# Filters loaded without a hold, other warm-up matmuls, and a feed-forward in 47 blocks of 512 tokens

## The chip, the cores and the metric

The kernel runs on one core of one Trainium2 chip. The metric is device time in microseconds (us). Before the change: 983.06 us, the median of ten runs (981.53 to 984.56).

## The reference

```python
def _attn_ref(x, filt_r, filt_i):               # x: 8 x 3008 x 256, filters: 1505 x 256
    X = np.fft.rfft(x, axis=1)
    F = (filt_r + 1j * filt_i)[None, :, :]
    return np.fft.irfft(X * F, n=x.shape[1], axis=1)

def _moe_ref(x, w_gate, w_val, w_out):          # 24064 tokens, d_model 256, d_ff 1536
    gate = np.maximum(x @ w_gate, 0.0)
    val = x @ w_val
    return gate * val @ w_out
```

The second takes the first one's result as 24064 x 256. Inputs and output are float32.

## The kernel before

**The transform.** A sequence of 3008 is taken as N1 x N2 = 94 x 32, token = n1 * 32 + n2, and done in stages for each of 8 batches.
- Stage A (`items_a`, L243 to L249): a DFT over n1. 16 items, each two float32 matmuls psA of 512 columns from x in SBUF (`XF`, two halves of 16 n2 each), one copy to `asb` on ScalarE. Every fourth item stores its `asb` to DRAM (`Abuf`) by the SP queue. `load_at` reads `Abuf` back in another order into `at`, one of four slabs of 32 partitions each. This is the first bounce.
- Stage B (`items_b`, L274 to L298): 12 items of a forward matmul pair psX, products with the filters on VectorE (`tt`, `uu`), and, two items late, an inverse of four matmuls psD, copied to `dsb` on ScalarE; two more items finish the inverses. Four stores (five in batch 0) put `dsb` into DRAM (`Dbuf`). `load_d` reads it back in eight tiles `dC`, each with four values of n2. Every tile needs all the stores. This is the second bounce.
- Stage C (`item_c`, L328): the DFT back over n1 by matmuls of 94 columns, psY, copied to `yT`, the feed-forward's input.

**The feed-forward** goes in blocks. A block takes one `dC` tile: four n2, all n1, 376 tokens, and 12 steps, one for each 128 columns of d_ff. In a step `gv` (L345 to L350) makes psV and psG with two matmuls each of 376 columns, ScalarE copies psV to `vsb`, and VectorE makes `prod` of psG and `vsb`. In the same step `o_part` (L365) does three matmuls psO of 256 columns for the block before: 128, 128 and 120 tokens in turn. After its steps 7 and 11 psO is copied and written by one transfer of SP's queue: 256 rows of 1 KB, then 120. `item_c` for the next block is called after steps 6 and 10.

**The order** is written by hand; each engine runs its instructions in the order of the program. The batch ahead is worked on beside the blocks: `side` holds what is called after which step (counted from the start of the batch's 96 steps). Stage A begins at step 5 (20 for batch 1), one item a step; stage B at step 35 (51), one item every two steps; `load_d` at step 66 (82). `load_x` for the batch after that is issued by POOL as soon as stage A has read a half of `XF`.

**The prologue** does batch 0 alone. x is loaded by SP, filters by POOL (`load_filters`, 20 transfers), after a hold: `hold_gpsimd` is a small copy on POOL that waits for a given tile, here for the first x. `place_filters` copies rows within SBUF, the first half on VectorE, the second by SP's transfers. Feed-forward weights come in three parts (`load_vg`) and `load_o`, by POOL: the first two parts after a hold on the third slab of `at`, the third after a hold on the first `dC`. `warm` issues junk matmuls of 512 columns, psJ, in stage A (one an item), after it (20), in stage B (two an item) and after it (26).

Of the kernel before, what the change touches and what calls it, by code (L numbers as in the profile page):

```python
# [13 lines left out]
BF16 = mybir.dt.bfloat16  # L14
# [13 lines left out]
N1, N2 = 94, 32  # L28
NROW = 96
NG = 24  # L30
S = N1 * N2
# [8 lines left out]
def _tables():  # L40
# [10 lines left out]
    lo = 32 * (lo % 32 // 8) + 8 * (lo // 32) + lo % 8  # L51
    i2t = np.zeros((128, NG, 64))
    i2u = np.zeros((128, NG, 64))
    perm = np.arange(N2) // 4 + 8 * (np.arange(N2) % 4)
    perm = np.concatenate([perm, 32 + perm])
    for hg in range(48):
        g, a = divmod(hg, 2)
        rows = slice(a * 64, a * 64 + 64)
        f = np.zeros((64, 64))
        t = np.zeros((64, 64))  # L60
        u = np.zeros((64, 64))
        k1 = 2 * hg + 2 if hg < 23 else 0 if hg == 23 else 2 * (hg - 24) + 1
        th = 2 * np.pi * ((n1 * k1) % N1) / N1
        wa[part, 2 * hg] = np.cos(th)
        if k1 not in (0, 47):
            wa[part, 2 * hg + 1] = -np.sin(th)
            m1[2 * hg] = 2.0 * np.cos(th) / S
            m1[2 * hg + 1] = -2.0 * np.sin(th) / S
            k = np.stack([k1 + N1 * p, S - (N1 * (p + 1) - k1)], 1).reshape(32)
            conj = np.tile([1.0, -1.0], 16)  # L70
            th = 2 * np.pi * (np.outer(n2, k) % S) / S
            c, s = np.cos(th), np.sin(th)
            f[:] = np.block([[c, -s], [s, c]])
            ct, st = c.T, s.T
            t[:] = np.block([[ct, st], [-st, ct]])
            u[:] = np.block([[-st, ct], [-ct, -st]]) * np.concatenate([conj, conj])[:, None]
        else:
            m1[2 * hg] = np.cos(th) / S
            th = 2 * np.pi * (np.outer(n2, k1 + N1 * p) % S) / S
            c, s = np.cos(th), np.sin(th)  # L80
            f[0:32, 0:32:2] = c
            f[0:32, 32::2] = -s
            t[0:32:2, 0:32] = 2.0 * c.T
            t[32::2, 0:32] = -2.0 * s.T
            u[0:32:2, 0:32] = -2.0 * s.T
            u[32::2, 0:32] = -2.0 * c.T
            if k1 == 0:
                sign = np.where(n2 % 2 == 0, 1.0, -1.0)
                f[0:32, 32] = sign
                t[0, 0:32] = 1.0  # L90
                t[32, 0:32] = sign
                u[0] = 0.0
                u[32] = 0.0
        f2[lo + 16 * a, g] = f
        i2t[rows, g], i2u[rows, g] = t[:, perm], u[:, perm]
    tab = np.stack([f2, i2t, i2u], 1).reshape(128, 3, 2, NG // 2, 64).transpose(0, 2, 1, 3, 4)
    return wa.astype(np.float32), m1.astype(NBF16), np.ascontiguousarray(tab).astype(NBF16)

# [2 lines left out]
def kernel(  # L101
# [15 lines left out]
    NC2 = 8  # L117
    NX2 = 16
    NZ = 8
    W = S // NZ  # L120

    wa_h, m1_h, tab_h = _tables()

# [132 lines left out]
    ats = {}  # L256
# [62 lines left out]

    yTs = {}  # L320

    def item_c(b, z, h):

        if h == 0:
            yTs[b, z] = sb.tile([128, 2, N1, 4], BF16, tag="yT", bufs=3, name="yT")
        psY = ps.tile([128, W], FP32, tag=fft_tag(), name="psY")
        for j in range(4):
            nc.tensor.matmul(psY[:, j * N1:(j + 1) * N1],  # L328
                             dCs[b, z][:, j, h * 128:(h + 1) * 128], M1,
                             start=True, stop=True)  # L330
        dst = yTs[b, z][:, h]
        src = psY.rearrange("p (b a) -> p a b", a=N1)
        if h == 0:
            nc.scalar.copy(dst, src)  # L334
        else:
            nc.vector.tensor_copy(dst, src)  # L336


    def gv(blk, ft, prods):
        yt = yTs[blk].rearrange("p h a b -> p h (a b)")  # L340
        psV = ps.tile([128, 512], FP32, tag="psv", name="psV")
        psG = ps.tile([128, 512], FP32, tag="psg", name="psG")
        for (pt, w) in ((psV, WvT), (psG, WgT)):
# [11 lines left out]

    def o_part(blk, s, prods):

        b, z = blk
        t = s // 4
        tw = min(128, W - t * 128)  # L360
        if s in (0, 8):
            ost["ps"] = ps.tile([128, 2, D], FP32, tag="pso", name="psO")
        psO = ost["ps"]
        for ft in range((s % 4) * 3, (s % 4) * 3 + 3):
            nc.tensor.matmul(psO[:tw, t % 2], prods[ft][:, t * 128:t * 128 + tw], WoT[:, ft, :],  # L365
                             start=(ft == 0), stop=(ft == NFT - 1))
        if s in (7, 11):
            n = 2 if s == 7 else 1
            osb = fs.tile([128, 2, D], FP32, tag="osb", bufs=3)
            nc.scalar.copy(osb[:tw, :n], psO[:tw, :n])  # L370
            r0 = b * S + (t + 1 - n) * 128 * NZ + z
            nc.sync.dma_start(_ap(out, r0 * D, [[NZ * D, tw], [128 * NZ * D, n], [1, D]]),
                              osb[:tw, :n])


    junk = pro.tile([128, 512], BF16, tag="junk", bufs=1)

    def warm(n):

        psJ = ps.tile([128, 512], FP32, tag=fft_tag(), name="psJ")  # L380
        for i in range(n):
            nc.tensor.matmul(psJ, junk[:, 0:128], junk, start=True, stop=True)  # L382

    nc.sync.dma_start(WA, nc.inline_tensor(wa_h, name="dft_wa").ap())
    q = NX2 * D // 4
# [10 lines left out]
    for (src, dst) in FILT:  # L396
        for g in (H - 1, NG - 1):
            nc.vector.memset(dst[64:128, g, :], 0.0)
    hold_gpsimd(XF[0][0:32, 0:8])
    load_filters(0)  # L400
    load_filters(1)

    warm(14)
    for i, f in enumerate(items_a(0)):
        f()
        warm(1)
        if i == 0:
            load_tables()
        if i % 4 == 3 and i > 3:
            load_at(0, i // 4 - 1)  # L410
    load_at(0, 3)
    warm(20)
    place_tables(0)
    place_filters(0)
    place_tables(1)
    place_filters(1)
    hold_gpsimd(ats[0][64:96, NG - 1, 0:8])
    load_vg(0)
    load_vg(1)

    for f in items_b(0, 2):
        f()
    warm(26)
    load_d(0)
    hold_gpsimd(dCs[0, 0][0:32, 0, 0:8])
    load_vg(2)
    load_o()
    load_x(1, nc.gpsimd)
    for h in range(2):
        item_c(0, 0, h)  # L430
    prologue.close()
    fs = ctx.enter_context(tc.tile_pool(name="fs", bufs=2))

    turn["tags"] = ("fft",)
    blocks = [(b, z) for b in range(B) for z in range(NZ)]
    prev = None
    for bi, blk in enumerate(blocks):
        b, z = blk
        if z == 0 and b + 1 < B:
            side = {}  # L440

            def at_step(s, f):
                side.setdefault(s, []).append(f)
            s0 = 5 if b else 20
            for i, f in enumerate(items_a(b + 1)):
                at_step(s0 + i, f)
            for c in range(4):
                at_step(s0 + 7 + 4 * c, lambda b=b, c=c: load_at(b + 1, c))
            if b + 2 < B:
                at_step(s0 + 19, lambda b=b: load_x(b + 2, nc.gpsimd))  # L450
            sb0 = (s0 + 30) | 1
            for i, f in enumerate(items_b(b + 1)):
                at_step(sb0 + 2 * i, f)
            at_step(sb0 + 31, lambda b=b: load_d(b + 1))
        elif z == 0:
            side = {}
        prods = []
        for ft in range(NFT):
            gv(blk, ft, prods)
            if prev is not None:  # L460
                o_part(prev[0], ft, prev[1])
            for f in side.get(z * NFT + ft, ()):
                f()
            if ft in (6, 10) and bi + 1 < len(blocks):
                item_c(*blocks[bi + 1], 0 if ft == 6 else 1)
        prev = (blk, prods)
    for s in range(NFT):
        o_part(prev[0], s, prev[1])
# [28 lines left out]
```

## Time and profile before

| | |
|---|---|
| median of ten runs | 983.06 us |
| the profiled execution | 983.94 us |
| its span | 982.2 us |
| stage A of batch 0, first psA to last | 8.06 to 25.04 us |
| first psX of batch 0 | 37.02 us |
| end of stage B of batch 0 | 54.07 us |
| first psV of the feed-forward | 60.57 us |
| one batch, first psA of batch 6 to that of batch 7 | 116.9 us |
| last psO ends, end of span | 978.6 us, 982.2 us |

The span is the time from the first to the last instruction of the program. PE is the matrix engine, PEld its weight loads, DVE VectorE, ACT ScalarE, POOL GpSimd, SP the queue that issues most transfers. A line of the timeline gives start, duration, engine, source line, operation, output<-inputs, shape, count; matmuls overlap, so their pace is the distance between starts. A line of the window view gives, for each engine, its busy time and instructions in that stretch, then the TensorE clock that was granted, the busy share of the DMA engines and GB/s.

These are the transfers around the change, as the page lists them (KB each, median us from issue to landing):

```profile
out_dram<-osb SPq DMA_DIRECT2D x64, 256.0 KB, 2.2
Abuf<-asb SPq DMA_DIRECT2D x32, 384.0 KB, 4.9
at<-Abuf SPq DMA_DIRECT2D x32, 384.0 KB, 7.7
dC<-Dbuf SPq DMA_DIRECT2D x64, 192.0 KB, 4.4
Dbuf<-dsb SPq DMA_DIRECT2D x31, 384.0 KB, 2.8
out_dram<-osb SPq DMA_DIRECT2D x64, 120.0 KB, 1.9
```

### The profile page before, as it was taken

What the parts mean: (1) busy time and instruction counts of PE and PEld (TensorE: products, weight loads), DVE (VectorE), ACT (ScalarE), POOL (GpSimd) and SP (SyncE); (2) the same over time, 40 slices, a digit from 0 to 9 for tenths busy, and PEclk for the clock granted to TensorE, in tenths of its full rate; (3) what the DMA queues carried; (4) which work ended last, traced back from release to release, by engine and by line L of the source; (5) the groups of instructions that cost most, each with busy time, mean ns of one, the idle gap of its engine ahead of it and who ended that gap; (6) DMA issues with size and microseconds to landing.
All of it is one profiled execution on the core that took longest, in us unless ns stands there. A gap on an engine that the chain in (4) does not pass through costs nothing.

```text
span 982.2 us, 18335 instructions
## 1 busy us (share of the span) xinstructions
PE 964.4 (98%) x6820; PEld 665.1 (68%) x6820; DVE 577.0 (59%) x1046; ACT 556.8 (57%) x1191; POOL 51.9 (5%) x86
## 2 busy tenths in 40 slices
PE   8689999999999999999999999999999999999998
PEld 3345677657775677757776577765777667777776
DVE  4534487438754496536855378543875449655554
ACT  4245556556655556555665556555665555655554
POOL 5430000010000000000000000001000000000000
PEclk9899999999999999999999999999999999999999
DMA  9993924183322814146230652317432142411111
GB/s 263 199 212 124 246 59 136 45 226 83 105 67 63 243 54 129 32 129 177 75 113 21 172 135 81 112 44 214 92 101 73 55 118 59 129 33 33 33 33 48
DMA packets 96825, 107.20 MB, mean 109 GB/s; under 512 B 6212, under 2 KB 85508, under 8 KB 95108
## 3 DMA queue, kind: packets, MB, share of 16 engines
q1 hardware_dynamic: 87760, 78.97, 29.0%
q0 software_dynamic: 8576, 25.86, 10.5%
q8 instruction: 53, 0.87, 0.4%
q10 hardware_dynamic: 400, 1.20, 0.3%
q14 instruction: 36, 0.29, 0.1%
HBM read 59.31 MB, written 49.81 MB: 111 GB/s over the span
## 4 chain that ended last, share of the span: by engine, by line
PE 96%; DMA 2%; issue 1%; DVE 0%; POOL 0%; ACT 0%; DVEq 0%; POOLq 0%; ACTq 0%
PE psO L365 26%; PE psG L345 25%; PE psV L345 25%; PE psA L243 11%; PE psX L274 2%; PE psY L328 2%; PE psD L294 2%; PE psD L293 2%; PE psJ L382 1%; DMA WgT<-in_moe_w_gate_dram 1%; DMA Abuf<-asb 1%; DMA at<-Abuf 1%; POOL uu L281 0%; DVE XF L386 0%; DVE uu L283 0%
## 5 line engine op out<-in xcount | busy, mean ns | idle before, releaser
L350 DVE SCALAR_TENSOR_TENSOR prod<-psG,vsb 128x376 bf16<-128x376 f32 x768 | 421.3, 550 | 361.5 <-ACT vsb L348 348.2
L348 ACT CAST vsb<-psV 128x376 bf16<-128x376 f32 x768 | 363.5, 473 | 213.8 <-PE psV L345 211.2
L365 PE MATMUL psO<-WoT,prod 128*128 128x256 bf16 (+1 forms) x2304 | 375.1, 273 | 0.0
L345 PE MATMUL psV<-yT,WvT 128*128 128x376 bf16 x1536 | 371.1, 323 | 2.2 <-DMA WvT<-in_moe_w_val_dram 1.6
L345 PE MATMUL psG<-yT,WgT 128*128 128x376 bf16 x1536 | 370.7, 323 | 0.7 <-DMA WgT<-in_moe_w_gate_dram 0.7
L365 PEld LDWEIGHTS <-prod 128*128 128x128 bf16 (+1 forms) x2304 | 246.1, 110 | 89.9
L345 PEld LDWEIGHTS <-WgT 128*128 128x128 bf16 x1536 | 149.8, 98 | 96.9 <-issue 1.4
L345 PEld LDWEIGHTS <-WvT 128*128 128x128 bf16 x1536 | 143.4, 98 | 69.2 <-issue 55.5
L246 ACT CAST asb<-psA 96x512 bf16<-96x512 f32 x128 | 74.4, 582 | 100.8 <-PE psA L243 99.5
L243 PE MATMUL psA<-XF,WA 128*96 128x512 f32 x256 | 130.7, 592 | 0.0
L296 ACT CAST dsb<-psD 128x512 bf16<-128x512 f32 x96 | 56.2, 587 | 51.0 <-PE psD L294 49.6
L370 ACT COPY osb<-psO 128x512 f32<-128x512 f32 (+1 forms) x128 | 61.6, 481 | 19.9 <-PE psO L365 13.7
L277 DVE TENSOR_TENSOR tt<-psX,Ftr 128x512 bf16<-128x512 f32 x96 | 65.4, 682 | 10.0 <-PE psX L274 10.0
L283 DVE TENSOR_TENSOR uu<-psX,Fti 128x512 bf16<-128x512 f32 x90 | 61.3, 681 | 0.0
L154 POOL DMA_DIRECT2D XF<-in_x_dram x42 | 21.6, 522 | 598.0 <-PE psA L243 580.6
L294 PE MATMUL psD<-uu,I2u 128*128 128x256 bf16 x192 | 47.3, 273 | 1.2 <-POOL uu L281 1.2
L293 PE MATMUL psD<-tt,I2t 128*128 128x256 bf16 x192 | 47.6, 274 | 0.0
L328 PEld LDWEIGHTS <-dC 96*128 96x128 bf16 x512 | 35.8, 97 | 14.9 <-issue 12.4
L274 PE MATMUL psX<-at,F 128*128 128x256 bf16 x192 | 37.3, 277 | 7.5 <-DMA at<-Abuf 7.5
L328 PE MATMUL psY<-M,dC 96*128 96x94 bf16 x512 | 42.3, 204 | 0.0
L336 DVE CAST yT<-psY 128x376 bf16<-128x376 f32 x64 | 34.6, 541 | 12.1 <-PE psY L328 12.1
L334 ACT CAST yT<-psY 128x376 bf16<-128x376 f32 x64 | 30.2, 472 | 19.6 <-PE psY L328 19.6
(45 smaller groups left out, 184.9 us busy)
## 6 DMA issues: line engine op xcount, KB each, us to landing
XF<-in_x_dram POOLq DMA_DIRECT2D x40, 512.0 KB, 6.7
out_dram<-osb SPq DMA_DIRECT2D x64, 256.0 KB, 2.2
Abuf<-asb SPq DMA_DIRECT2D x32, 384.0 KB, 4.9
at<-Abuf SPq DMA_DIRECT2D x32, 384.0 KB, 7.7
dC<-Dbuf SPq DMA_DIRECT2D x64, 192.0 KB, 4.4
Dbuf<-dsb SPq DMA_DIRECT2D x31, 384.0 KB, 2.8
out_dram<-osb SPq DMA_DIRECT2D x64, 120.0 KB, 1.9
XF<-in_x_dram SPq DMA_DIRECT2D x6, 256.0 KB, 4.1
```

The costliest lines, as they stand in the source:

```text
L243: nc.tensor.matmul(psA[0:NROW], WA[:, :NROW], XF[c * NC2 // NX2][:, o:o + 512], start=True, stop=True)
L246: nc.scalar.copy(dst, psA[0:NROW])
L277: nc.vector.tensor_tensor(tt, psX, Ftr[:, g:g + 2, :], op=ALU.mult)
L283: nc.vector.tensor_tensor(uu, psX, Fti[:, g:g + 2, :], op=ALU.mult)
L293: nc.tensor.matmul(psD[:, i], I2t[:, g + i, :], tt[:, i], start=True, stop=False)
L294: nc.tensor.matmul(psD[:, i], I2u[:, g + i, :], uu[:, i], start=False, stop=True)
L328: nc.tensor.matmul(psY[:, j * N1:(j + 1) * N1], dCs[b, z][:, j, h * 128:(h + 1) * 128], M1, start=True, stop=True)
L345: nc.tensor.matmul(pt[:, :W], w[:, h, ft * 128:(ft + 1) * 128], yt[:, h, :], start=(h == 0), stop=(h == 1))
L348: nc.scalar.copy(vsb, psV[:, :W])
L350: nc.vector.scalar_tensor_tensor(prod, in0=psG[:, :W], scalar=0.0, in1=vsb, op0=ALU.max, op1=ALU.mult)
L365: nc.tensor.matmul(psO[:tw, t % 2], prods[ft][:, t * 128:t * 128 + tw], WoT[:, ft, :], start=(ft == 0), stop=(ft == NFT - 1))
L370: nc.scalar.copy(osb[:tw, :n], psO[:tw, :n])
```

## The change

In the prologue: the hold ahead of the filters is gone; the junk matmul in each item of stage A has 256 columns; 26 junk matmuls follow stage A and 28 follow stage B, one goes with each item of stage B; the hold ahead of the first weights is on the fourth slab of `at`; the third part of the value and gate weights is issued after the fifth item of stage B.

In the loop: tokens are taken in order of batch, n2, n1, and cut into 47 blocks of 512, across n2 and across batches. `runs` gives the pieces of a stretch of tokens that share an n2: `item_c` issues one psY for each piece, `o_part` one output transfer for each piece of a tile of 128 tokens. A step has matmuls of 512 columns in `gv` and four psO of 128 tokens; psO is copied for two tiles at a time, after steps 5 and 11, and tile by tile in the last block. Steps are counted over the whole loop. `item_c` follows steps 7 and 10. The tables' order of n2 loses its permutation, and psY is copied without rearrangement.

```diff
-        i2t[rows, g], i2u[rows, g] = t[:, perm], u[:, perm]
+        i2t[rows, g], i2u[rows, g] = t, u
...
-    W = S // NZ
+    W = 512
+    NB = B * S // W
...
+    def runs(t, n):
+        o = 0
+        while o < n:
+            b, r = divmod(t + o, S)
+            n2, n1 = divmod(r, N1)
+            w = min(N1 - n1, n - o)
+            yield o, b, n2, n1, w
+            o += w
...
-        for j in range(4):
-            nc.tensor.matmul(psY[:, j * N1:(j + 1) * N1],
-                             dCs[b, z][:, j, h * 128:(h + 1) * 128], M1,
+        for (o, b, n2, n1, w) in runs(k * W, W):
+            nc.tensor.matmul(psY[:, o:o + w],
+                             dCs[b, n2 // 4][:, n2 % 4, h * 128:(h + 1) * 128], M1[:, n1:n1 + w],
                              start=True, stop=True)
...
-        t = s // 4
-        tw = min(128, W - t * 128)
-        if s in (0, 8):
+        t = s // 3
+        if s in (0, 6):
...
-        for ft in range((s % 4) * 3, (s % 4) * 3 + 3):
+        for ft in range((s % 3) * 4, (s % 3) * 4 + 4):
...
-        if s in (7, 11):
-            n = 2 if s == 7 else 1
+        last = blk == NB - 1
+        if s in (5, 11) or last and s % 3 == 2:
+            t0 = t if last else t - 1
...
-            r0 = b * S + (t + 1 - n) * 128 * NZ + z
-            nc.sync.dma_start(_ap(out, r0 * D, [[NZ * D, tw], [128 * NZ * D, n], [1, D]]),
-                              osb[:tw, :n])
+            for tt in range(t0, t + 1):
+                for (o, b, n2, n1, w) in runs(blk * W + tt * 128, 128):
+                    nc.sync.dma_start(_ap(out, (b * S + n1 * N2 + n2) * D, [[N2 * D, w], [1, D]]),
+                                      osb[o:o + w, tt % 2])
...
-    hold_gpsimd(XF[0][0:32, 0:8])
     load_filters(0)
...
-        warm(1)
+        warm(1, 256)
...
-    warm(20)
+    warm(26)
...
-    hold_gpsimd(ats[0][64:96, NG - 1, 0:8])
+    hold_gpsimd(ats[0][96:128, NG - 1, 0:8])
...
-    for f in items_b(0, 2):
+    for i, f in enumerate(items_b(0, 1)):
         f()
-    warm(26)
+        if i == 4:
+            load_vg(2)
+    warm(28)
...
-    load_vg(2)
     load_o()
...
+    LAST = 9
+    for b in range(1, B):
+        end = (b * S // W - 1) * NFT + LAST - 5
+        if b == 1:
+            s0, sb0 = 13, 33
+            every = [sb0 + i + i // 2 for i in range(14)]
+        else:
+            s0 = end - 54
+            every = [(s0 + 24 | 1) + 2 * i for i in range(14)]
+        for i, f in enumerate(items_a(b)):
+            at_step(s0 + i, f)
+        for c in range(4):
+            at_step(s0 + 6 + 4 * c, lambda b=b, c=c: load_at(b, c))
+        if b + 1 < B:
+            at_step(s0 + 17, lambda b=b: load_x(b + 1, nc.gpsimd))
+        for i, f in zip(every, items_b(b)):
+            at_step(i, f)
+        at_step(every[-1] + 1, lambda b=b: load_d(b))
```

So batch 1 has its stage A at steps 13 to 28, the last `load_at` at 31, stage B at 33 to 52 (two items in three steps), `load_d` at 53, and its first token in block 5, whose `item_c` follows steps 55 and 58. A later batch has 25 steps from its first psA to its first psX and six from its last item of stage B to the `item_c` that first reads its `dC`. Block 5 is the last 448 tokens of batch 0 and 64 of batch 1.

## The prediction

> **What bounds the kernel now.** I read the busy shares, then the slices, then the main loop as one window, to see whether any engine other than PE ever sets the time.
>
> ```profile
> PE 964.4 (98%) x6820; PEld 665.1 (68%) x6820; DVE 577.0 (59%) x1046; ACT 556.8 (57%) x1191; POOL 51.9 (5%) x86
> PE   8689999999999999999999999999999999999998
> 90.00:982.00 892.00, 888.60 (x6445) 625.41 (x6443) 535.03 (x973) 520.49 (x1122) 18.43 (x36) 1.00 0.36 99
> ```
>
> From 90 us on PE is never idle until the last output is written. So the loop is worth what its matmuls cost, and all DMA time is hidden: by a margin that has to be found. PE's pace comes from its timeline, start to start:
>
> ```profile
> 41.55 0.38 PE L274 MATMUL psX<-at,F 128*128 128x256 bf16 x2
> 41.77 0.59 PE L382 MATMUL psJ<-junk 128*128 128x512 bf16 x2
> 42.20 0.27 PE L293 MATMUL psD<-tt,I2t 128*128 128x256 bf16 x1
> ...
> 692.54 0.48 PE L345 MATMUL psG<-yT,WgT 128*128 128x376 bf16 x2
> 692.86 0.49 PE L365 MATMUL psO<-WoT,prod 128*120 128x256 bf16 x3
> 693.18 0.48 PE L345 MATMUL psV<-yT,WvT 128*128 128x376 bf16 x2
> ```
>
> 256 columns take 0.109 us, 376 take 0.16 (0.159 over the whole trace), 512 take 0.216; 128x120 weights cost as much as full ones. The bounce through DRAM, in the timeline of the SP queue and the DMA view of the same 13 us:
>
> ```profile
> 330.50 0.30 SPq L248 DMA_DIRECT2D Abuf<-asb  x1
> 330.85 0.42 SPq L261 DMA_DIRECT2D at<-Abuf  x1
> 335.40 0.32 SPq L261 DMA_DIRECT2D at<-Abuf  x1
> ...
> 379.08 0.37 SPq L298 DMA_DIRECT2D Dbuf<-dsb  x1
> 381.83 4.07 SPq L317 DMA_DIRECT2D dC<-Dbuf  x8
> ```
>
> ```profile
> q1 hardware_dynamic: 2012, 1.50, 47.9%
> q0 software_dynamic: 144, 1.57, 41.6%
> ```
>
> The last psA ends at 329.85; store 330.50, last at load 335.40, landed 343.0, first psX 344.66. From the last store of D to the first dC in SBUF: 379.08 to 384.4. Both fit now, the first with 1.7 us to spare. Of the DMA engines' 12.9 us, x takes 5.4 and SP's queue 6.2.
>
> The prologue has idle PE and half clock (windows; columns PE busy, clock, DMA share, GB/s):
>
> ```profile
> 34.60:38.00 3.40, 0.98 (x4) 0.50 1.15 243
> 65.30:68.70 3.40, 1.46 (x11) 1.00 1.26 186
> 68.70:72.10 3.40, 2.99 (x10) 0.51 1.41 275
> ```
>
> Last, one 120-row output transfer alone:
>
> ```profile
> DMA packets 135, 0.12 MB, mean 61 GB/s; under 512 B 15, under 2 KB 135, under 8 KB 135
> ```
>
> 120 rows and 15 small packets: it ran on 15 engines. The 256-row one shows 272 packets, 256+16, at 33.9% of 16 engines over 2.3 us: 48 ns a row.
>
> **The Trainium skill.** (1) "DMA: Bandwidth & Descriptors", section "Why a DMA increments its semaphore by 16 and not by 1": a transfer runs on the largest number of engines up to 16 that divides its slowest dimension, on SP's queue the lowest-numbered ones. The 135 packets agree on the number; no run here shows which engines. (2) Same page, "Queues, rings and completion order": each engine takes one queue's descriptors in ring order and alternates between queues. The second at load landing last agrees. (3) "TensorE: Matmul & The Clock Gate", "What's actually happening": the clock halves after a mostly idle window of 3413 ns, and windows are free-running. The trace agrees: 6.8 and 3.4 us at 0.50. (4) Same page, "Wait — 56ns, not 53.3ns?": about 2.5 ns per matmul beside its columns; 0.216 for 512 agrees.
>
> **PE work.** psO: 47 blocks x 48 = 2256 matmuls for 2304: 48 x 0.109 = -5.2. gv: 2256 x 0.216 = 487.3 for 3072 x 0.159 = 488.4: -1.1 (-1.8 at the page's 215.7 ns). psY: 604 for 512, same columns: 92 x 2.5 ns = +0.2, at most 92 x 0.04 = 3.7 if a short one costs a full one; I take the small end. Evictions of 512 (0.59 on ACT as for asb, about 0.69 on DVE as for tt) fit in a step of 4 x 0.216 + 4 x 0.109 = 1.30. Sum -6.3.
>
> **Prologue.** Stage A: the junk is halved, 16 x 0.107 = -1.7. But filters now start when POOL's memsets end (4.3) rather than at 8.06, beside x. XF's second half, landed at 15.4 (issue 8.30 + 7.1), would be needed at 15.8. The DMA engines are full from 4 us on, so a delay of over 0.4 us comes back. I take -1.0, from -1.7 to +1.5. Bounce: store 5.6 plus load 5.5 beside filter traffic that now ends earlier, while the SBUF copies now come wholly beside the load: -1.0 (-3 to +1). The 26 junk matmuls still end about 6 us before psX, so a half window stays. Stage B (37.02 to 54.07): dropping 12 junk pairs matters only in the first four items, at half clock; later pairs of items (42.64, 44.89, 47.23) are held by psX, tt 0.69, xs 0.59, POOL's uu 1.15. The two inserted POOL issues (0.73 each) mostly fit its 1.1 us gaps. -1.3 (-2.5 to +0.8). Block 0 needs the second dC tile, 0.8 us after the first, and the junk is 0.43 longer: +0.4. Earlier third weights: waits of 1.77 and 0.92 go, and the half window after them, 3.08 us for work of 1.59: -4.2; the load then lies beside the near-empty DMA of stage B. WoT and x follow 3.4 us of DMA time less, so x(1) comes about at step 13. Sum -7.1.
>
> **The crossing, batch 1.** Block 5 ends in batch 1, so its data is due at step 55, not 90. In t from the end of the last psA (step 28): psX comes after steps 29 to 33, 5 x 1.30 + 0.3 for psY = 6.8. Before, it needed 13.1. The earlier issue of load 2 helps: the store goes at 0.65 and lands at 5.5 (4.9 as before). x keeps about three quarters of an engine while it runs (before, the store's 1 us of engine time took 4.9 beside it), so its 5.4 us last from 1.3 to 8.4. Without outputs the last load, 1.9 us of engine time, has 0.8 by then, ends at 9.5 and lands by 10.2: wait 3.4.
>
> But the outputs change. 128 transfers become 440, most by rows of 94 = 2 x 47: two engines. Counting divisors, the first two engines carry 6704 rows each, 28% of 24064, where each carried a sixteenth. A group (two tiles, 4 or 5 transfers) puts 21 to 128 rows, 71 on average, on engine 0: 3.4 us. Step 29's group (73 rows, 3.5 us) is issued at 2.2 to 4.4, ahead of the last load in the ring. From 5.3 to 8.4 the ring gets 0.8 us, then 2.7 + 1.9 to 13.0, 0.7 to land and start: 13.7. Wait 6.9 (3.4 to 8.5), plus a half window, on average 1.6.
>
> Then dC: last inverse at step 52, load at 53, psY at the end of 55: 3.9 + 0.2. Store issue at 1.0, landed 3.7, but step 53's outputs stand in front of load_d on SP (2.2 to 4.2, then 0.45 an issue) and 87 rows, 4.2 us, on the ring until 7.1; the tile's 0.7 and landing 0.6 give 8.4. Wait 4.4 (3.1 to 5.5), with clock 1.5. Late x(1): 0.2. Sum +14.6.
>
> **Later batches.** psX has 10 steps, 13.5. The same sum with the group of s0+13 ahead gives 12.6 for 58 rows, 13.7 for 85, 15.8 for 128 (batch 3): +2.6. dC has 6 steps, 7.8, for 0.9 + 2.75 + 0.1 + 2.9 = 6.7; a group of 87 rows adds 1.1: +0.5. Sum +3.1 (0 to 15).
>
> **The end.** Now PE ends 3.5 us before the span does. After: four tiles put 46, 50, 21, 64 rows on engine 0; the first becomes available 2.4 us before PE ends, the last 1.55 after, done at about 6.1, landed 6.5; then 1.2 as now: 7.7. +4.2 (0.5 to 5).
>
> **Sum.** -6.3 - 7.1 + 14.6 + 3.1 + 4.2 = +8.5. Against the profiled execution, 983.94 (span 982.2): 992.4; that run is 0.9 above the median, so 983.06 + 8.5 = 991.6.
>
> **Rivals.**
> - Outputs do not hinder (rows spread over engines, or their rings drain in time). For it: DMA share is 0.36 in the loop, and mean load of engines 0 and 1 stays under full. Against: 15 for 120. Then batch 1 costs 3.4 + 1.6 + 3.1 + 1.3 + 0.2 = 9.6, later ones 0.3, the end 0.5: -13.4 + 10.4 = -3.0, 980.1. This one is not slower; it decides once a group takes less than about 1 us on its busiest engine.
> - Every batch waits: x keeps three quarters of each engine and groups over 80 rows come up in most bounces, so six batches lose 2 us more each, idle and clock: +20, 1003. For it: slack is near 0 in my own sums. Against: three of the groups are below 76 rows.
> - The change doesn't do what it says: filters delay x and hand back the prologue, 2 to 3 us more; inside the ranges.
>
> **How the numbers follow.** Forecast 0.50 (own range 986 to 997), no hindrance 0.28 (975 to 986), every batch 0.22 (997 to 1010). About 0.2%, 2 us, can be told from no change. Faster, under 981.1, is a little over half of the second case: 0.16; same, to 985.0, its rest and little else: 0.13; slower 0.71. Leaving out a tenth on each side: 979 to 1003.
>
> **What would show it.** Right: PE idle before the first psX of batch 1 by 5 to 8 us, before block 5's psY by 3 to 5, each followed by a clock of 0.5; output landings of 3 to 8 us rather than 2.2; last PE to end of span 7 to 8 us; no wait for WvT or WgT at 66 us. Wrong: landings near 2.2 us and PE full from 90 us on.

## The result, and the profile after

The changed kernel takes 1012.99 us (median of 9 runs, 1012.02 to 1017.16) where the kernel before takes 982.91 (median of 31): ratio 1.0309, 95% interval 1.0299 to 1.0319. The profiled executions, 1012.84 against 983.94, have spans of 1011.1 and 982.2 us: 28.9 us more where 8.5 were forecast. "Slower" was right; 20.4 us were missing from the size. The nine runs spread over 5 us, and most experiments below are a single execution, so small differences between them are read from the traces and not from the times.

The first part of the page and its slices, of the kernel after:

```profile
PE 961.5 (95%) x6044; PEld 566.4 (56%) x6044; DVE 545.9 (54%) x825; ACT 522.0 (52%) x938; POOL 51.2 (5%) x85
...
PE   8699797999999999999999999999999999999995
...
PEclk9799898999999999999999999999999999999999
```

PE still sets the time, but there are now two dips near 120 and 170 us, each with a lower clock, and the last slice is half empty. What shows in no slice is spread thin. The groups of the kernel after (busy, mean ns, then the idle time before them and who ended most of it):

```profile
L372 PE MATMUL psO<-WoT,prod 128*128 128x256 bf16 x2256 | 337.7, 273 | 2.5 <-ACT osb L378 2.5
...
L243 PE MATMUL psA<-XF,WA 128*96 128x512 f32 x256 | 130.2, 593 | 2.2 <-DMA XF<-in_x_dram 1.4
...
L274 PE MATMUL psX<-at,F 128*128 128x256 bf16 x192 | 38.1, 281 | 15.3 <-DMA Fti<-Fti 7.5
...
L338 PE MATMUL psY<-M,dC 96*128 96x94 bf16 (+18 forms) x604 | 37.8, 199 | 14.8 <-ACT dsb L296 9.4
```

psY had no idle time before it in the kernel before; now it has 14.8 us, and 9.4 of it ends with ScalarE's copy of psD. No step of the forecast has that releaser. The two waits that were forecast stand in PE's timeline (start, duration; in brackets the idle time and what ended it):

```profile
124.07 0.61 PE L274 MATMUL psX<-at,F 128*128 128x256 bf16 x2 [6.75 <-DMA at<-Abuf]
...
170.47 0.24 PE L338 MATMUL psY<-M,dC 96*128 96x64 bf16 x1 [5.40 <-DMA dC<-Dbuf]
```

and the windows around them have half the clock (PE busy, PEld, DVE, ACT, POOL, then clock, DMA share, GB/s):

```profile
120.00:123.40 3.40, 0.00 (x0) 0.00 (x0) 0.00 (x0) 0.00 (x0) 0.00 (x0) 0.50 0.52 138
123.40:126.80 3.40, 2.73 (x9) 1.34 (x10) 1.59 (x3) 0.58 (x1) 0.00 (x0) 0.50 0.00 0
167.80:171.20 3.40, 0.73 (x3) 0.34 (x4) 0.00 (x0) 0.46 (x1) 0.00 (x0) 0.50 0.89 260
171.20:174.60 3.40, 3.40 (x11) 1.51 (x10) 0.69 (x1) 1.16 (x3) 0.00 (x0) 0.50 0.33 110
```

SP's queue in front of them, where the forecast expected outputs to stand ahead of the bounce:

```profile
111.24 0.30 SPq L248 DMA_DIRECT2D Abuf<-asb  x1
112.54 3.61 SPq L381 DMA_DIRECT2D out_dram<-osb  x5
119.38 0.33 SPq L261 DMA_DIRECT2D at<-Abuf  x1
...
162.91 1.86 SPq L381 DMA_DIRECT2D out_dram<-osb  x5
164.88 5.55 SPq L317 DMA_DIRECT2D dC<-Dbuf  x8
```

The last load of `at` is issued 8.14 us after the store it needs, and within 0.02 us of that store's landing. So the outputs issued in between didn't keep the load back in SP's order; the store itself landed late (the page of before has a median of 4.9 us for these stores). Before dC it is otherwise: `load_d` goes out right behind the outputs. The end, all engines:

```profile
1000.54 0.37 ACT L378 COPY osb<-psO 128x256 f32<-128x256 f32 x1 [2.47 <-DMA out_dram<-osb]
...
1000.97 1.47 PE L372 MATMUL psO<-WoT,prod 128*128 128x256 bf16 x12 [1.99 <-ACT osb L378]
```

The last block copies its four tiles one by one into three `osb` buffers. The third copy (1000.54) waits 2.47 us for the landing of an earlier output, and PE waits for that copy; the fourth waits 2.19 us in the same way. That the last outputs run on two engines shows in the DMA view of 1004.0 to 1008.4 us, when PE is done (queue: packets, MB, share of 16 engines):

```profile
q1 hardware_dynamic: 199, 0.19, 12.6%
```

12.6% of 16 is 2.0 engines.

**Where the 28.9 us are.** I go through PE's instructions of both traces from start to start, take each one's columns at full pace off, and sort the rest by place. Forecasts are put on the same footing (the prologue's -7.1 without its third weights is -2.9; late x goes with psX).

| part, after minus before, us | forecast | measured |
|---|---|---|
| start to first psV (60.57 to 62.72) | -2.9 | +2.15 |
| third weights, their waits and half window | -4.2 | -4.3 |
| columns of the matmuls | -6.3 | -7.1 |
| wait before psX of batch 1, with clock | +8.7 | +8.7 |
| wait before psY of block 5, with clock | +5.9 | +7.6 |
| psX and the rest, later batches | +3.1 | +2.2 |
| psY behind psD in one step, 14 times 0.84 | none | +11.7 |
| psO behind osb in the last block | none | +2.8 |
| last psO to end of span (3.57 to 8.62) | +4.2 | +5.05 |
| sum | +8.5 | +28.8 |

Two rows lean on one execution. The start scatters: thirteen runs with the change's prologue have the first psV between 61.2 and 62.8 us, median 61.7; the three with the old one have 60.6, 60.7 and 61.3. The two compared here lie at the ends, and about 1 us of the 2.15 is typical. The third weights cost 4.3 us in the profiled execution of the kernel before, but 1.6 and 1.4 in the two later traces with the same prologue, which show no half clock there. And 0.3 ns in the pace of a matmul of 512 columns moves 0.7 us between "columns" and "later batches".

### The profile page after: what moved, and what is told of

Read it like the earlier page. It is cut to its first block, busy times and chain, and to the rows that moved or that the text cites. A ratio compares the mean times of both kernels' runs of the same rounds, so it can differ in the third digit from the quotient of the medians.

```text
span 1011.1 us, 16316 instructions
## 1 busy us (share of the span) xinstructions
PE 961.5 (95%) x6044; PEld 566.4 (56%) x6044; DVE 545.9 (54%) x825; ACT 522.0 (52%) x938; POOL 51.2 (5%) x85
## 4 chain that ended last, share of the span: by engine, by line
PE 91%; DMA 5%; ACT 1%; POOL 1%; DVE 1%; SPq 1%; issue 0%; POOLq 0%; ACTq 0%
PE psV L354 24%; PE psG L354 24%; PE psO L372 24%; PE psA L243 10%; PE psY L338 2%; PE psX L274 2%; PE psD L294 2%; PE psD L293 2%; DMA Abuf<-asb 1%; DMA XF<-in_x_dram 1%; ACT dsb L296 1%; PE psJ L391 1%; DMA out_dram<-osb 1%; DMA dC<-Dbuf 1%; DMA at<-Abuf 0%
## 5 line engine op out<-in xcount | busy, mean ns | idle before, releaser
L359 DVE SCALAR_TENSOR_TENSOR prod<-psG,vsb 128x512 bf16<-128x512 f32 x564 | 390.0, 691 | 397.2 <-ACT vsb L357 380.9
L357 ACT CAST vsb<-psV 128x512 bf16<-128x512 f32 x564 | 331.1, 587 | 222.2 <-PE psV L354 150.6
L372 PE MATMUL psO<-WoT,prod 128*128 128x256 bf16 x2256 | 337.7, 273 | 2.5 <-ACT osb L378 2.5
L354 PE MATMUL psV<-yT,WvT 128*128 128x512 bf16 x1128 | 337.4, 380 | 0.9 <-DVE yT L345 0.5
L354 PE MATMUL psG<-yT,WgT 128*128 128x512 bf16 x1128 | 336.8, 380 | 0.0
L372 PEld LDWEIGHTS <-prod 128*128 128x128 bf16 x2256 | 220.9, 98 | 147.5 <-issue 4.4
L354 PEld LDWEIGHTS <-WgT 128*128 128x128 bf16 x1128 | 110.2, 98 | 135.4 <-issue 3.0
L354 PEld LDWEIGHTS <-WvT 128*128 128x128 bf16 x1128 | 104.3, 98 | 66.5 <-issue 55.5
L283 DVE TENSOR_TENSOR uu<-psX,Fti 128x512 bf16<-128x512 f32 x90 | 61.3, 681 | 0.0
L338 PE MATMUL psY<-M,dC 96*128 96x94 bf16 (+18 forms) x604 | 37.8, 199 | 14.8 <-ACT dsb L296 9.4
L345 DVE CAST yT<-psY 128x512 bf16<-128x512 f32 x47 | 32.1, 684 | 17.3 <-PE psY L338 17.2
```

The lines of the kernel that those rows point to most:

```text
L283: nc.vector.tensor_tensor(uu, psX, Fti[:, g:g + 2, :], op=ALU.mult)
L338: nc.tensor.matmul(psY[:, o:o + w], dCs[b, n2 // 4][:, n2 % 4, h * 128:(h + 1) * 128], M1[:, n1:n1 + w], start=True, stop=True)
L354: nc.tensor.matmul(pt[:, :W], w[:, h, ft * 128:(ft + 1) * 128], yt[:, h, :], start=(h == 0), stop=(h == 1))
L357: nc.scalar.copy(vsb, psV[:, :W])
L359: nc.vector.scalar_tensor_tensor(prod, in0=psG[:, :W], scalar=0.0, in1=vsb, op0=ALU.max, op1=ALU.mult)
L372: nc.tensor.matmul(psO[:, t % 2], prods[ft][:, t * 128:(t + 1) * 128], WoT[:, ft, :], start=(ft == 0), stop=(ft == NFT - 1))
```

## The experiments

### One step of the loop: psY behind psD

The timeline of the kernel after, at one of the 14 places:

```profile
252.16 0.38 PE L274 MATMUL psX<-at,F 128*128 128x256 bf16 x2
...
252.70 0.27 PE L294 MATMUL psD<-uu,I2u 128*128 128x256 bf16 x1
...
253.01 0.58 ACT L296 CAST dsb<-psD 128x512 bf16<-128x512 f32 x1 [0.94 <-PE psD L294]
...
253.65 0.39 PE L338 MATMUL psY<-M,dC 96*128 96x92 bf16 x6 [0.67 <-ACT dsb L296]
```

psX, psD and psY share one PSUM tag with two buffers (`fft_tag`). Stage B stands at odd steps; `item_c` followed steps 6 and 10 and now follows 7 and 10. At step 7 psY is the third tile in one step: it waits until ScalarE has read psD, 0.84 us more than the pace from psD to psY. The same place in the kernel before, where psY came a step after psD:

```profile
235.21 0.27 PE L294 MATMUL psD<-uu,I2u 128*128 128x256 bf16 x1
236.28 0.33 PE L328 MATMUL psY<-M,dC 96*128 96x94 bf16 x4
```

The theory was tried from both sides. In the changed kernel, `item_c` was put at even steps:

```diff
-            if ft in (LAST - 2, LAST + 1) and k + 1 < NB:
-                item_c(k + 1, 0 if ft < LAST else 1)
+            if ft in (8, 10) and k + 1 < NB:
+                item_c(k + 1, 0 if ft == 8 else 1)
```

> The changed kernel with item_c after steps 8 and 10 of a block instead of 7 and 10; stage B's items stand at odd steps. Theory 'same step' (a psY that follows a psX and psD in its own step must wait for dsb's copy, 14 waits of 0.84 us): they go, -11.7, and batch 1's wait for dC is one step shorter, -1.3: about 1000 us. Rival 'the wait only moves' (ACT or VectorE are late anyway, and the next psX or psY pays): within 3 us of 1013.

Measured: 1000.73, 12.3 us less. Of the 14 waits one is left, in batch 1, whose stage B doesn't keep to odd steps. And in the kernel before, this alone:

```diff
-            if ft in (6, 10) and bi + 1 < len(blocks):
-                item_c(*blocks[bi + 1], 0 if ft == 6 else 1)
+            if ft in (7, 10) and bi + 1 < len(blocks):
+                item_c(*blocks[bi + 1], 0 if ft == 7 else 1)
```

> The kernel before with the first item_c of a block after step 7 instead of 6; stage B's items stand at odd steps. Theory 'same step': 14 times a psY now follows psX and psD in its step and waits some 0.7 to 0.9 us for dsb's copy: +10 to +12, about 993. Rival 'the wait belongs to blocks of 512': no change, 982.

Measured: 993.85 against 982.15 beside it, +11.7, with 14 waits that sum to 11.72. Its group:

```profile
L328 PE MATMUL psY<-M,dC 96*128 96x94 bf16 x512 | 42.2, 204 | 9.4 <-ACT dsb L296 9.4
```

The same 9.4 as after the whole change (idle time; 11.7 from start to start), so this is shown: one call moved by one step costs 11.7 us.

### The outputs: rows on two engines, or many transfers

Each copy of psO as one transfer:

```diff
-            for tt in range(t0, t + 1):
-                for (o, b, n2, n1, w) in runs(blk * W + tt * 128, 128):
-                    nc.sync.dma_start(_ap(out, (b * S + n1 * N2 + n2) * D, [[N2 * D, w], [1, D]]),
-                                      osb[o:o + w, tt % 2])
+            n = t + 1 - t0
+            nc.sync.dma_start(_ap(out, (blk * W + t0 * 128) * D, [[D, 128], [128 * D, n], [1, D]]),
+                              osb[:, t0 % 2:t0 % 2 + n])
```

> The changed kernel with each copy of psO written by one transfer of 256 (128) rows on 16 engines; the rows go to the output in the order of the blocks, so their places differ. Theory 'two engines' (rows of 94 crowd the rings of engines 0 and 1): psX of batch 1 waits 3.5 instead of 7.0, dC 3 instead of 5.6, batch 3's 1.3 goes, and the end shrinks from 8.6 plus 3.0 of idle PE to 4 us: -15, about 998 us. Rival 'the bounces are late by themselves': the two waits of batch 1 stay within 1 us and only the end gains: 1004 to 1006.

Measured: 996.68, 16.3 us less than the change. PE's timeline has:

```profile
121.30 0.38 PE L274 MATMUL psX<-at,F 128*128 128x256 bf16 x2 [4.60 <-DMA at<-Abuf]
164.20 0.20 PE L338 MATMUL psY<-M,dC 96*128 96x64 bf16 x1 [2.00 <-DMA dC<-Dbuf]
```

With clock, batch 1's two waits cost 6.5 and 2.3 instead of 8.7 and 7.6, batch 3's wait is gone, psO loses 1.3 in the last block (both waits are for the copies of single tiles, none for a landing) and the end is 3.7 us, about as before the change.

That takes away both the narrow pieces and their number. To part them, two kernels with 256-row copies cut in other ways:

```diff
+                for (p0, p1) in ((0, 122), (122, 128)):
...
+                cuts = (0, 48, 128) if tt % 2 == 0 else (0, 32, 80, 128)
+                for (p0, p1) in zip(cuts, cuts[1:]):
```

> The changed kernel with each tile of psO written by two transfers, 122 rows (2 x 61, two engines) and 6, in the order of the blocks, so the rows' places differ: 376 transfers instead of 440, but 12032 rows on each of engines 0 and 1 instead of 6704. Theory 'two engines': batch 1's waits are at least 7 and 5.6, more batches wait before psX, and the end, 256 rows on engine 0, takes 12 us or more: over 1018. Rival 'the number of transfers on SP's queue': waits a little under those of the changed kernel, 1005 to 1012.

> The changed kernel with each copy of psO written by five transfers of 48, 80, 32, 48 and 48 rows, all on 16 engines, in the order of the blocks, so the rows' places differ: 470 transfers instead of 440. Theory 'two engines': as with one transfer a copy, 996 to 999, batch 1's waits 4.9 and 2.3. Rival 'the number of transfers on SP's queue' (each issue 0.4 us, and every ninth waits for the landing of the first): batch 1's waits stay at 7 and 5, only the end gains: 1003 to 1008.

Measured: 1050.3 with 376 transfers of which half have 122 rows (2 x 61), 1000.56 with 470 transfers of 32, 48 and 80 rows. Fewer transfers than the change's 440 cost 53.6 us more than one a copy; more of them, in multiples of 16, cost 3.9, all but about 0.6 of it in batch 1. So the number of rows in a transfer decides, as the page "DMA: Bandwidth & Descriptors" of the Trainium skill has it (section "Why a DMA increments its semaphore by 16 and not by 1": the largest divisor up to 16 is the number of engines). By that rule the first two engines carry 11656 rows each in the run with 122 rows; the 12032 of its forecast counts the pieces of six rows as if they ran on two. These three runs also put the rows of a block side by side in the output, where the change puts them 32 KB apart; both kinds of cut have that in common, so it doesn't explain their difference. In the run with 122 rows a bounce waits in every batch (psX in six of the seven, psY in all):

```profile
L274 PE MATMUL psX<-at,F 128*128 128x256 bf16 x192 | 38.2, 282 | 31.3 <-DMA at<-Abuf 18.6 <-DMA Fti<-Fti 7.1 <-issue 5.7
L338 PE MATMUL psY<-M,dC 96*128 96x94 bf16 (+18 forms) x604 | 39.5, 200 | 23.2 <-DMA dC<-Dbuf 13.8 <-ACT dsb L296 9.4
```

This is the rival "every batch waits", brought about with more narrow rows than the change has. Narrow pieces in the kernel before, where the crossing has all its slack:

```diff
-            nc.sync.dma_start(_ap(out, r0 * D, [[NZ * D, tw], [128 * NZ * D, n], [1, D]]),
-                              osb[:tw, :n])
+            for j in range(n):
+                cut = (94 if j == 0 else 62) if n == 2 else 60
+                for (p0, p1) in ((0, cut), (cut, tw)):
+                    nc.sync.dma_start(_ap(out, (r0 + (128 * j + p0) * NZ) * D,
+                                          [[NZ * D, p1 - p0], [1, D]]),
+                                      osb[p0:p1, j])
```

> The kernel before with each output transfer cut by rows into pieces of 94 and 34, 62 and 66, 60 and 60: 384 transfers, and engines 0 and 1 carry 6976 rows each (6704 in the changed kernel). Theory 'two engines and SP's queue crowd the bounces': psX of some batches waits (slack 1.7 us), 0 to 2 us for each of 7 batches, and the end grows by 1: 984 to 994. Rival 'the crossing in batch 1 alone makes them count': within 1.5 us of the kernel before.

Measured: 991.27 against 982.15. psX waits 6.1 us over five batches, and the end grows from 3.6 to 7.4 us. Waits and end come without any new crossing.

Last, the change's own pieces, each cut at its last multiple of 16:

```diff
+                    for (c, m) in ((0, w // 16 * 16), (w // 16 * 16, w % 16)):
+                        if m:
+                            nc.sync.dma_start(_ap(out, (b * S + (n1 + c) * N2 + n2) * D,
+                                                  [[N2 * D, m], [1, D]]),
+                                              osb[o + c:o + c + m, tt % 2])
```

> The changed kernel with each piece of rows cut at the last multiple of 16, so that most rows go on 16 engines: 784 output transfers instead of 440. Theory 'two engines': it gains nearly as much as one transfer a copy, less the issue of 344 more transfers on SP (0.4 us each, partly ahead of load_d): 999 to 1004. Rival 'the number of transfers on SP's queue': no better than 1013, rather 1016.

Measured: 1008.96, between the two. The end falls to 6.5 us and batch 3's wait goes, but batch 1 waits 8.2 and 4.7 us. SP's waits between 105 and 125 us show a second way in which outputs can delay a bounce (for whom, on what: us, times, longest):

```profile
SPq L261 <- DMA Abuf<-asb: 4.5, 1, 4.5
SPq L383 <- DMA Abuf<-asb: 3.1, 1, 3.1
```

An output (L383) waits 3.1 us for the landing of the store `Abuf`, with whose data it has nothing to do. In the trace it counts on the semaphore that this store used eight transfers earlier. The last load of `at` stands behind it on SP. It needs the same store, which landed at 118.23, and goes out at 119.51: 1.3 us are lost in SP's order. With the change's 440 transfers it was 0.02 us.

### x beside the bounce, and the queue that issues outputs

The runs of the next two sections have `item_c` at steps 8 and 10, so their base is 1000.73. First, outputs by POOL:

```diff
-                    nc.sync.dma_start(_ap(out, (b * S + n1 * N2 + n2) * D, [[N2 * D, w], [1, D]]),
+                    nc.gpsimd.dma_start(_ap(out, (b * S + n1 * N2 + n2) * D, [[N2 * D, w], [1, D]]),
```

> The changed kernel with item_c after steps 8 and 10 and the output transfers issued by POOL instead of SP, pieces as they are. Theory 'two engines': wherever they are issued, rows of 94 still go on two engines, so the end stays 7 to 9 us and batch 1's waits fall little: 996 to 1000. Rival 'SP's queue' (the stores, loads and dC stand behind the outputs there): batch 1's waits fall to 3.5 and 3 as with one transfer a copy, 990 to 993.

Measured: 985.49, better than both. psX of batch 1 waits 0.9 us, its dC 1.7, and the end, from PE to the end of the span, is 5.4 us instead of 8.9. That rows of 94 go on two engines from any queue is refuted: in the DMA view of 980.2 to 981.2 us 0.12 MB, nearly all of the last 128 rows (34 and 94), go by in 1 us,

```profile
q0 software_dynamic: 75, 0.12, 41.0%
```

which is 6.6 engines on average. But POOL issues x too, in order behind outputs: all six x transfers left at 114.3 to 117.4, after the last load of the bounce at 113.16; in the base, three left from 92.05 on and three from 109.83 on. So the run changes more than the order on SP. One kernel delays x alone:

```diff
+            if b == 1:
+                at_step(s0 + 19, lambda: nc.gpsimd.tensor_copy(
+                    sb.tile([32, 8], BF16, tag="scx", bufs=1, name="scx"), ats[1][96:128, NG - 1, 0:8]))
+            at_step(s0 + (19 if b == 1 else 17), lambda b=b: load_x(b + 1, nc.gpsimd))
```

> The changed kernel with item_c after steps 8 and 10, and the x of batch 2 held on POOL until the last slab of batch 1's at has landed, so that no x lies beside that bounce; outputs stay on SP's queue. With x in the way the wait before batch 1's psX was 7.4 us and the time 1000.7. If x's delay alone was what made the run with outputs on POOL fast there (it was delayed there too), the wait falls under 1.5 us and the time to 991 to 993, with the dC wait of 4.4 us unchanged. If the outputs on two engines hold up the last load by themselves, 3 to 5 us of wait stay and the time is 996 to 999. The dC wait and the end (8.9 us after the last psO) should not move by either theory.

Measured: 995.74. PE's timeline has

```profile
119.56 0.39 PE L274 MATMUL psX<-at,F 128*128 128x256 bf16 x2 [2.92 <-DMA at<-Abuf]
...
164.78 0.23 PE L338 MATMUL psY<-M,dC 96*128 96x64 bf16 x1 [3.84 <-DMA dC<-Dbuf]
```

Start to start, 7.4 us before psX became 3.2: x held up the first bounce by 4.2 us, and what stays is there without x. With wide outputs and x in place (996.68 above, `item_c` after 7 and 10) 4.9 of 7.0 stayed. Each of the two accounts for a part; neither does for all. The second bounce has no x beside it and hardly moved (4.3 to 4.0).

SP's timeline tells where the time went. With wide outputs, then with x late:

```profile
110.61 0.30 SPq L248 DMA_DIRECT2D Abuf<-asb  x1
115.82 0.32 SPq L261 DMA_DIRECT2D at<-Abuf  x1
...
110.55 0.30 SPq L248 DMA_DIRECT2D Abuf<-asb  x1
114.54 0.33 SPq L261 DMA_DIRECT2D at<-Abuf  x1
```

From the last store to its load it is 5.2 and 4.0 us, where the changed kernel has 8.1 and the base of this section 8.3. From the load to psX it is 5.5 and 5.0, where they have 4.7 and 4.9. So narrow outputs and x hold up the store, not the load; why a store that was issued ahead of the outputs lands later for them, no run here shows.

Another kernel takes the outputs out of SP's order alone:

```diff
-                    nc.sync.dma_start(_ap(out, (b * S + n1 * N2 + n2) * D, [[N2 * D, w], [1, D]]),
+                    nc.scalar.dma_start(_ap(out, (b * S + n1 * N2 + n2) * D, [[N2 * D, w], [1, D]]),
```

> The changed kernel with item_c after steps 8 and 10, and every output transfer issued by ACT's queue in place of SP's: pieces and their places stay, so they should still run on few engines, but nothing of SP's stands behind them. If order in SP's queue was the cause of the waits (bounce transfers standing behind outputs), the wait before batch 1's psX falls from 7.4 to under 2 us, that before its psY from 4.4 to under 1, and the time to 987 to 990 (end unchanged, 8.9 us). If the rows on two engines were the cause, at most 2 us of each wait goes and the time is 996 to 1001; ACT's issues, about 0.3 us each and on the path of vsb, can add some us to either.

Measured: 1064.11, which neither theory gave. ScalarE itself is held up, and PE with it:

```profile
L357 ACT CAST vsb<-psV 128x512 bf16<-128x512 f32 x564 | 325.2, 590 | 250.5 <-PE psV L354 121.3 <-DMA out_dram<-osb 70.5 <-DVE prod L359 29.3
```

For 70.5 us vsb stands behind output issues that wait for earlier outputs to land. Batch 1's waits became 3.6 and 3.0, but in a schedule that these stalls had shifted, so this run doesn't say how much SP's order by itself is worth. The base does: its last load of `at` leaves at 118.48, 0.01 us after the store's landing, so nothing is lost there. Its `load_d` leaves 3.3 us after the last store of D, behind the outputs, where 2.8 us are enough with wide outputs: about 0.5 us, an estimate from these two traces.

### More time for batch 1

```diff
-            s0, sb0 = 13, 33
+            s0, sb0 = 13, 31
...
-            at_step(s0 + i, f)
+            at_step(s0 + (i // 2 if b == 1 else i), f)
...
-            at_step(s0 + 6 + 4 * c, lambda b=b, c=c: load_at(b, c))
+            at_step(s0 + (4 + 2 * c if b == 1 else 6 + 4 * c), lambda b=b, c=c: load_at(b, c))
```

> The changed kernel with item_c after steps 8 and 10 and, in batch 1 alone, two items of stage A a step (13 to 20), load_at at 17 to 23, stage B at 31 to 50. Theory 'batch 1 is late because stage A ends at step 28': with 11 steps, 14 us, between the last psA and the first psX and 5 to 6 between the last inverse and dC, the waits of 7 and 4.5 us and their half windows (6.8 us each, 3.4 lost) go: -15 to -17, 984 to 986. Rival 'x or the queues hold it up all the same': 995 or more.

> Both of the others of this call together. If the crossing of batch 1 and the step phase are the causes and outputs on POOL help the end or the bounces: 980 to 985, at best under the kernel before. If POOL's outputs hold the loads of x up: 988 or more.

Measured: 991.15 with outputs on SP, and 984.23 with this and POOL's outputs together. The dC wait is gone in the first, while psX still waits 3.0 us with a half window after it, although its stage A is done earlier. In the second run batch 1 waits no more for transfers, and what is left is psX in later batches, 4.0 us, and the end.

### The prologue

The prologue's part of the change in the kernel before (the edit below), and in another run the third weights alone:

```diff
-    hold_gpsimd(XF[0][0:32, 0:8])
...
-        warm(1)
+        warm(1, 256)
...
-    warm(20)
+    warm(26)
...
-    hold_gpsimd(ats[0][64:96, NG - 1, 0:8])
+    hold_gpsimd(ats[0][96:128, NG - 1, 0:8])
...
-    for f in items_b(0, 2):
+    for i, f in enumerate(items_b(0, 1)):
         f()
-    warm(26)
+        if i == 4:
+            load_vg(2)
+    warm(28)
...
-    load_vg(2)
```

> The kernel before with the prologue part of the change alone: no hold ahead of the filters, the hold on the fourth slab, 256-column junk in stage A, 26 and 28 junk matmuls after A and B, one an item in B, the third weights after the fifth item of B. Theory: the prologue gives back in stage A and the first bounce what half-width junk saves (first psV at 61 to 62 us for 60.6), and saves the 4.2 of waits and half clock for the third weights: 979 to 980. Rival 'the early weights are of no use in this order' (WoT or x late instead): 983 to 985.

> The kernel before with the third part of the value and gate weights issued after the fifth item of stage B, and nothing else. Theory: only the waits of 1.77 and 0.92 and the half window behind them go, first psV stays at 60.6: 978 to 979. Rival: the load or POOL's issues hold stage B up, first psV 61.5 or later: 980 and up.

Measured: 981.09 and 980.66, one run each, against 982.15. Runs of the kernel before spread from 981.3 to 984.9, so neither difference from it is sure; but in both traces the two waits for weights and the half window after them are gone, and against the profiled 983.94 the third weights alone are worth 3.3 of the 4.2 forecast. The rest of the prologue's edits show no gain: with them the first psV comes at 61.69, without at 61.26, which is within the scatter. What takes their place is in POOL's queue. Kernel after:

```profile
4.26 0.71 POOL L186 DMA_DIRECT2D Ftr<-in_filt_r_dram  x1
...
20.18 0.65 POOL L192 DMA_DIRECT2D Fti<-in_filt_i_dram  x1 [5.83 <-DVE F L171]
...
22.89 0.55 POOL L186 DMA_DIRECT2D Ftr<-in_filt_r_dram  x1
```

and kernel before:

```profile
8.06 0.72 POOL L186 DMA_DIRECT2D Ftr<-in_filt_r_dram  x1 [0.41 <-issue]
...
21.59 0.55 POOL L186 DMA_DIRECT2D Ftr<-in_filt_r_dram  x1
```

The first half of the filters sets off 3.8 us earlier, yet the second half sets off 1.3 us later. The DMA engines are full (share 1.04 to 1.24 from 8 to 24 us, in the kernel after): what the filters gain, x and the tables lose. In the kernel before with the prologue's part of the change the last of x lands at 17.7 us instead of 15.4, the last table at 21.2 instead of 19.4. POOL then waits for landings of its own: ahead of 20.18 for its third transfer (issued 5.51, landed 19.61; VectorE, which the line names, came 0.1 us after it), then for its fourth, which landed at 22.13 where the kernel before has 20.50. psA waits for x in the timeline of after:

```profile
18.28 1.07 PE L243 MATMUL psA<-XF,WA 128*96 128x512 f32 x2 [1.44 <-DMA XF<-in_x_dram]
```

The hold was put back into the changed kernel:

```diff
+    hold_gpsimd(XF[0][0:32, 0:8])
     load_filters(0)
```

> The changed kernel with the hold ahead of the filters put back. Theory 'filters beside x' (x's halves are late by 1.1 and 1.7 us in stage A, and the rest of the first bounce follows): first psA items without wait, first psX at 37 instead of 39.3: -2 to -3, about 1010.5. Rival 'the DMA engines have the same work before psX either way': first psX within 0.7 us of 39.3, 1012 to 1013.

Measured: 1013.14, no gain in all, though the first psX came at 37.68 instead of 39.31 and the first psV at 61.17 instead of 62.72. In all five runs that have the hold the first psX comes between 37.0 and 37.8 us, in all thirteen without it between 37.9 and 39.5; the medians are 0.9 apart. Four of the five have the old warm-up matmuls too, so that the hold alone is worth this is likely and not shown. What was gained there was given back in batch 1, where this run had 10.2 us at half clock around the first wait instead of 6.8.

### A version that beats both

```diff
-            s0, sb0 = 13, 33
-            every = [sb0 + i + i // 2 for i in range(14)]
+            s0 = 13
+            every = [30, 31, 33, 35, 36, 38, 39, 41, 42, 43, 45, 47, 48, 49]
...
-            s0 = end - 54
-            every = [(s0 + 24 | 1) + 2 * i for i in range(14)]
+            s0 = end - 58
+            every = [(s0 + 28 | 1) + 2 * i for i in range(14)]
...
-                    nc.sync.dma_start(_ap(out, (b * S + n1 * N2 + n2) * D, [[N2 * D, w], [1, D]]),
-                                      osb[o:o + w, tt % 2])
+                    c1 = w // 16 * 16 if last else w
+                    for j, (c, m) in enumerate(((0, c1), (c1, w - c1))):
+                        if m:
+                            eng = nc.sync if last and j == 0 else nc.gpsimd
+                            eng.dma_start(_ap(out, (b * S + (n1 + c) * N2 + n2) * D,
+                                              [[N2 * D, m], [1, D]]),
+                                          osb[o + c:o + c + m, tt % 2])
```

with `item_c` after steps 8 and 10 and batch 1's stage A two items a step as above; later batches have four steps more for their first bounce.

> The changed kernel with item_c after steps 8 and 10; batch 1's stage A two items a step, its stage B at hand-picked steps from 30 to 49, never 8 or 10 of a block; later batches' stage A four steps earlier; outputs issued by POOL, those of the last block cut at multiples of 16 and shared between SP and POOL. If the step phase, batch 1's crossing and the outputs' queue and engines are the causes, only the prologue's loss and some 2 us at the end remain: 974 to 977, faster than the kernel before. If POOL's outputs or the earlier stage A bring waits of their own: 981 or more.

Measured: 977.75 (977.54 to 978.25, 4 runs) against 982.81; ratio 0.9943, interval 0.9926 to 0.9959: about half a per cent faster than the kernel before. PE hardly waits from the crossing on until the last block (window view; first PE, last clock 1.00):

```profile
116.00:232.00 116.00, 116.00 (x747) 69.77 (x746) 68.25 (x105) 64.35 (x117) 32.38 (x64) 1.00 0.42 133
```

psY's idle time is 0.1 us in all. The end keeps 5.0 us after the last psO and 1.6 of waits before it, and that is what the expectation missed.

## Why the prediction was right or wrong

- **The third weights and the columns.** Right in place and size for the executions compared: -4.3 for -4.2, -7.1 for -6.3.
- **psX of batch 1.** Right in its causes, x and narrow outputs, but +8.7 for +8.7 is luck. The forecast had the last store land 4.9 us after its issue and put the outputs in the way of the load, 8.2 us from there to psX. The trace has 8.1 us for the store and 4.7 from the load to psX; one error of 3.2 and one of 3.5 cancel. The sum's own wait without the output group was 3.4 us; with wide outputs 4.6 were measured.
- **dC of batch 1.** Right mechanism, undersized: idle 5.4 rather than 4.4, and 2.0 for the clock rather than 1.5. `load_d` left 3.3 us after the store, as forecast (3.2), but the tile then took 5.5 us instead of 4.2.
- **Later batches.** +2.2 for +3.1. The forecast put 2.3 in batch 3; there was 1.3.
- **"PE work" failed.** Its line on psY priced 604 matmuls at +0.2, at most 3.7, by their columns and starts alone, and for the loop only transfers were followed. That `item_c` follows step 7 instead of 6 was in the text on the change, and nothing was summed for it. A matmul moved by one step has to be followed to its PSUM buffer too: who else takes that tag in the new step, and who must read it out first. It cost 11.7 us, more than half of the 20.4 us by which the sum was short. (A slip of no weight: the terms as written, -5.2, -1.1 and +0.2, add to -6.1 and not to -6.3.)
- **"Prologue" failed.** Stage A -1.0 measured +1.1 (start of the last psA 24.44 to 25.53), the bounce -1.0 measured +1.2 (from there to the first psX, 12.58 to 13.78), stage B with block 0 -0.9 measured -0.15. The forecast itself noted that the engines are full from 4 us on; it should have followed that the filters' early start can then delay x, tables and with them POOL's later filters, by more than the 0.7 us it took from stage A's gain. These 5 us are the second largest error; about 1 of them is the scatter of the two executions.
- **"The end"** had 7.7 us from PE to the end, measured 8.6. It left out that PE waits in the last block, 2.8 us: 1.3 for the copies tile by tile, which stay with wide outputs, and 1.5 because the three `osb` buffers are freed by landings and these are slow.
- **The rivals.** "Outputs do not hinder" is refuted by the waits and by the narrow pieces in the kernel before (+9.1). "Every batch waits" didn't come about at the change's rows (71 on engine 0 in a group on average, by the forecast's count), but did with 122-row pieces (+53.6 over wide ones). Its number, 1003, was nearer to the result than the forecast was, for another reason.

## What to carry to other kernels

When a call moves by one step in a hand-written order, list what shares its PSUM tag in the new step before pricing the matmuls: here a two-buffer tag with three users in a step put an eviction on the path each time, 0.84 us and 14 times. Choose the rows of an output transfer for their divisors: on SP's queue, pieces in multiples of 16 rows cost 3.9 us here, fewer ones of twice a prime 53.6. Before starting a load earlier, look whether the DMA engines are full, as they were here; ask which other load it delays, and who waits for that.

## What the runs showed that was not expected

- Outputs on POOL's queue (440 issues, 228 us of POOL's time at 525 ns each) landed in a median 2.1 us where they had 94 rows, and the span ended 5.4 us after PE where it was 8.9 with SP's queue. POOL had the time to spare: 5% busy before.
- A queue can wait for a landing that its data doesn't need: an output waited 3.1 us for a store that had used its semaphore eight transfers before, with 784 output transfers.
- The same issues on ScalarE's queue stop ScalarE: 70.5 us of idle before vsb, 1064.11 us in all.
